# A transformer block with linear attention on one core: start-up loads on two queues, denominators spread by two loads a block, and a new order of instructions

## The chip, the core and the metric

The kernel runs on one core of a Trainium2 chip. A core has five engines that run side by side and meet through semaphores: TensorE (PE, matrix products; its weight loads, PEld, overlap them), VectorE (DVE), ScalarE (ACT), GpSimd (POOL) and SyncE (SP). Data come and go by DMA: SP, ACT and POOL each issue transfers from a queue of their own, and the core's 16 DMA engines carry them out. The metric is the device time of one execution in microseconds (us). The kernel before took 738.85 us (median of three runs, 738.4 to 741.09).

## The reference

One block of a transformer for 2,048 rows of width 1,024: a modulation vector from c, a normalized attention part with 32 heads of width 32 and linear attention, and a normalized feed-forward part of width 3,584. All arrays are bfloat16.

```python
x = A_x
mod = (silu(c) @ w_mod).reshape(c.shape[0], 6, 1, -1)
sa, ca, ga, sb, cb, gb = (mod[:, i] for i in range(6))
h = layernorm(x) * (1 + ca) + sa
# attention: q, k, v = h @ wqkv, 32 heads of width 32
#   pq, pk = phi(q), phi(k);  phi(t) = where(t > 0, t + 1, exp(t)) + 1e-6
#   kv = sum over rows of pk (outer) v;  z = sum over rows of pk
#   o = (pq @ kv) / (pq . z + 1e-6);  result = o @ wo
x = x + ga * attention(h)
h = layernorm(x) * (1 + cb) + sb
x = x + gb * ((gelu(h @ w_gate) * (h @ w_up)) @ w_down)
```

## The kernel before

**Tiling.** The 2,048 rows are four blocks of 512 rows (b = 0 to 3), each four tiles of 128 rows; the feed-forward part works on two groups of 1,024 rows. The width of 1,024 is eight column groups of 128 (`KD`), each with four heads. Most products of 512 rows or more are made with seven sub-products in place of eight (`seven`), which costs sums on VectorE.

**Who decides the order.** The kernel's text doesn't issue instructions. `Plan` records them, with their engine and what they read and write, and `order` then schedules each engine's list by a model of costs. After that `refine` moves each engine's instructions by the table `SHIFTS`: one number for each instruction, saying from how many places further on the one in this place is taken. `issue` emits the result. Each engine and each queue runs its list strictly in order, so an instruction that waits holds up all behind it.

**The start** (`start_phase`). SP loads four tiles of x (line 772), quarters of the weights Wv (line 776) and halves of two column sets of `w_mod` (line 939), after a first DMA for c (line 767). Tiles 0, 1 and 3 get their statistics on VectorE (`ln_rows`: two bn_stats, line 857, one bn_aggr, line 859, and Ln and Exp on ScalarE); tile 2 gets them on ScalarE (`act_stats`, lines 876 to 879). The tiles are normalized (lines 886 and 982), transposed on TensorE (`start_tile`, line 899), and copied to `hs0` (lines 902 and 903). Meanwhile c becomes `scol` (lines 965 to 971 and one product at line 779), and `scale_cols` (line 924) makes the columns `opcA` (line 927) by which `scale_wv` (line 907) scales Wv. Then the V products run (`v_plain`, line 915), and `keep_warm` (line 893) puts two products without a use in between. ScalarE's function table is loaded once, at line 759, before everything else on ScalarE.

**The denominators.** `den_sums(pr, ps)` makes the 32 heads' denominators for two blocks (pr 0: blocks 0 and 1; pr 1: blocks 2 and 3) with 16 small products (line 1271), turns them into reciprocals on ScalarE (lines 1273 and 1274) and stores them in DRAM (`den_scr`, four stores of 16 KB, line 1279). `den_mul(b)` loads them back with each head's row repeated on 32 partitions (line 1289) into `rden`, 128 x 8 x 512, and VectorE multiplies the block's `pqT[b]` by them, two column groups at a time (a product at line 779). Blocks 0, 1 and 2 share one buffer `rden`; block 3 has another.

**What follows.** `wo_tile` makes the output projection of blocks 0 and 1, tile by tile (16 products at line 1519, an addition to x at line 1521 that frees the banks); `wo_stages` makes blocks 2 and 3 with `seven` (line 1583). ScalarE and VectorE normalize each tile (line 1461), GpSimd stores it, SP loads it back transposed (line 1455), and the feed-forward part begins (lines 1698, 1709). In between TensorE makes modulation rows from `w_mod` (`ModSet`, loads at line 788, products at line 796).

The two parts of `den_mul` and `den_sums` that move data, as they stand:

```python
sy.dma_start(out=den_scr[pr][b, :, KH * half:KH * half + KH, 0:TG], in_=rdc[o:o + KH * P // DH, :])
...
for j in range(P // DH):
    src = den_scr[b // 2][b % 2, j][:, 0:TG]
    sy.dma_start(out=rden[DH * j:DH * j + DH], in_=src[None, :, :].to_broadcast((DH, KD, TG)))
```

Of the kernel before, what the change touches and what calls it, by code (L numbers as in the profile page):

```python
# [11 lines left out]
BF16 = mybir.dt.bfloat16  # L12
# [4 lines left out]
ACT_TABLE_LN_EXP = 6  # L17
# [4 lines left out]
        "z1 4 4 4 4 4 -5 -5 -5 -5 48 -1 -1 -1 -1 -1 -1 -1 -1 -1 -1 -1 -1 -1 -1 -1 -1 7 7 7 7 7 7 7 7 7 7 7 7 7 7 7 7 "  # L22
        "-17 -17 -17 -17 -17 -17 -17 -17 3 3 3 3 -5 -5 -5 -5 8 8 8 8 20 20 20 20 20 20 20 20 20 20 20 20 20 20 20 20 "
        "-20 -20 -20 -20 24 24 24 24 24 24 24 24 24 24 24 24 24 24 24 24 -28 -28 -28 -28 -28 -28 -28 -28 -44 -44 -44 "
        "-44 16 16 16 16 -36 -36 -36 -36 12 12 12 12 12 12 12 12 12 12 12 12 -8 -8 -8 -8 -36 -36 -36 -36 28 28 28 28 "
        "-40 -40 -40 -40 -4 -4 -4 -4 z16 -20 -20 -20 -20 z12 16 16 16 16 16 16 16 16 16 16 16 16 16 16 16 16 16 16 16 "
        "16 16 16 16 16 16 16 16 16 16 16 16 16 -24 -24 -24 -24 -24 -24 -24 -24 -40 -40 -40 -40 -40 -40 -40 -40 8 8 8 8 "
        "8 8 8 8 8 8 8 8 8 8 8 8 -16 -16 -16 -16 -16 -16 -16 -16 z8 16 16 16 16 16 16 16 16 16 16 16 16 16 16 16 16 -16 "
        "-16 -16 -16 -16 -16 -16 -16 8 8 8 8 52 -21 -21 -21 -21 -21 -21 -21 -21 -1 -1 -1 -1 -1 -1 -1 -1 11 11 11 11 11 "
        "11 11 11 28 28 28 28 19 19 19 19 11 11 11 11 20 20 20 20 -25 -25 -25 -25 -25 -25 -25 -25 -25 -25 -25 -25 8 8 8 "  # L30
        "8 8 8 8 8 25 25 25 25 25 25 25 25 13 13 13 13 -37 -37 -37 -37 -37 -37 -37 -37 -3 -3 -3 -3 25 25 25 25 25 25 25 "
        "25 25 25 25 25 25 25 25 25 -32 -8 -8 -8 -8 -32 -32 -32 -32 -40 -40 -40 -40 -16 -16 -16 -16 -12 -12 -12 -12 -20 "
        "-20 -20 -20 40 40 40 40 z4 -8 -8 -8 -8 -4 -4 -4 -4 -4 -4 -4 -4 -4 -4 -4 -4 20 20 20 20 -4 -4 -4 -4 -12 -12 -12 "
        "-12 -8 -8 -8 -8 -8 -8 -8 -8 -8 -8 -8 -8 36 36 36 36 -4 -4 -4 -4 -4 -4 -4 -4 z4 4 4 4 4 -12 -12 -12 -12 -8 -8 "
        "-8 -8 4 4 4 4 8 8 8 8 8 8 8 8 -12 -12 -12 -12 16 16 16 16 z4 12 12 12 12 12 12 12 12 -36 -36 -36 -36 -8 -8 -8 "
        "-8 -16 -16 -16 -16 12 12 12 12 4 4 4 4 -4 -4 -4 -4 8 8 8 8 -16 -16 -16 -16 -4 -4 -4 -4 4 4 4 4 -4 -4 -4 -4 z8 "
        "4 4 4 4 -4 -4 -4 -4 4 4 4 4 -4 -4 -4 -4 z16 4 4 4 4 24 24 24 24 24 24 24 24 -4 -4 -4 -4 -4 -4 -4 -4 -20 -20 "
        "-20 -20 28 28 28 28 20 20 20 20 32 32 32 32 -20 -20 -20 -20 -20 -20 -20 -20 -20 -20 -20 -20 -12 -12 -12 -12 "
        "-12 -12 -12 -12 -12 -12 -12 -12 28 28 28 28 4 4 4 4 -12 -12 -12 -12 -12 -12 -12 -12 16 16 16 16 -4 -4 -4 -4 "
        "-12 -12 -12 -12 12 12 12 12 -8 -8 -8 -8 z4 -20 -20 -20 -20 16 16 16 16 16 16 16 16 16 16 16 16 -8 -8 -8 -8 12 "  # L40
        "12 12 12 -12 -12 -12 -12 -24 -24 -24 -24 8 8 8 8 -20 -20 -20 -20 -4 -4 -4 -4 4 4 4 4 -4 -4 -4 -4 4 4 4 4 -4 -4 "
        "-4 -4 4 4 4 4 -4 -4 -4 -4 z8 32 32 32 32 32 32 32 32 32 32 32 32 -12 -12 -12 -12 -8 -8 -8 -8 -8 -8 -8 -8 -20 "
        "-20 -20 -20 60 60 60 60 60 60 60 60 -16 -16 -16 -16 -24 -24 -24 -24 8 8 8 8 8 8 8 8 8 8 8 8 -28 -28 -28 -28 "
        "-36 -36 -36 -36 -16 -16 -16 -16 -24 -24 -24 -24 8 8 8 8 -12 -12 -12 -12 -12 -12 -12 -12 -12 -12 -12 -12 -12 "
        "-12 -12 -12 12 12 12 12 12 12 12 12 12 12 12 12 12 12 12 12 -24 -24 -24 -24 -12 -12 -12 -12 12 12 12 12 -24 "
        "-24 -24 -24 16 11 11 11 11 -9 -9 -9 -9 -9 -9 -9 -9 9 9 9 9 z5 -14 -14 -14 -14 z24 6 6 6 6 -2 -2 -2 -2 -8 -8 "
        "z10 6 6 6 6 -4 -4 -4 -4 -4 -4 2 2 2 2 2 2 2 2 -8 1 1 1 1 1 1 7 7 7 7 -18 6 6 6 6 -8 -8 -8 -8 2 -9 -9 11 11 11 "
        "11 -4 z4 1 -9 -9 -9 -9 1 1 1 1 -9 32 32 32 32 32 32 32 32 32 32 32 32 32 32 32 32 48 48 48 48 48 48 48 48 24 "
        "24 24 24 -28 -28 -28 -28 -28 -28 -28 -28 -28 -28 -28 -28 -28 -28 -28 -28 -28 -28 -28 -28 4 4 4 4 4 4 4 4 4 4 4 "
        "4 -40 -40 -40 -40 -40 -40 -40 -40 -40 -40 -40 -40 z8 64 64 64 64 4 4 4 4 4 4 4 4 -12 -12 -12 -12 -12 -12 -12 "  # L50
        "-12 4 4 4 4 4 4 4 4 -12 -12 -12 -12 -12 -12 -12 -12 -4 -4 -4 -4 -4 -4 -4 -4 -4 -4 -4 -4 -4 -4 -4 -4 4 4 4 4 4 "
        "4 4 4 -12 -12 -12 -12 -12 -12 -12 -12 z16 8 8 8 8 8 8 8 8 -8 -8 -8 -8 -8 -8 -8 -8 4 4 4 4 -4 -4 -4 -4 z8 44 44 "
        "44 44 24 24 24 24 -8 -8 -8 -8 -8 -8 -8 -8 -4 -4 -4 -4 -12 -12 -12 -12 -4 -4 -4 -4 -12 -12 -12 -12 -8 -8 -8 -8 "
        "16 16 16 16 8 8 8 8 -12 -12 -12 -12 -12 -12 -12 -12 -12 -12 -12 -12 4 4 4 4 -4 -4 -4 -4 8 8 2 2 2 2 4 4 4 4 4 "
        "4 4 4 -14 -14 -14 -14 8 8 8 8 8 8 8 8 -4 -4 -4 -4 -12 -12 -12 -12 20 20 20 20 -4 -4 -4 -4 -4 -4 -4 -4 12 12 12 "
        "12 24 24 -2 -2 -2 -2 -10 -10 -10 -10 10 10 10 10 -22 -22 -22 -22 8 8 32 32 -6 -6 -6 -6 6 6 -16 -16 -16 -16 22 "
        "22 z2 -8 -8 -8 -8 -4 -4 -4 -4 z2 -6 -6 -6 -6 z2 -6 -6 -6 -6 z4 6 6 -2 -2 -2 -2 -2 -2 6 6 6 6 -2 -2 -2 -2 4 4 4 "
        "4 -12 -12 38 38 8 8 8 8 34 34 -4 -4 -4 -4 8 8 4 4 -14 -14 -22 -22 -6 -6 -6 -6 -2 -2 -2 -2 8 8 -22 -22 20 20 20 "
        "20 -6 -6 -12 -12 -12 -12 -10 -10 -10 -10 z6 4 4 4 4 -14 -14 -14 -14 z6 12 12 12 12 -4 -4 -4 -4 32 32 32 32 8 8 "
        "8 8 -12 -12 -12 -12 -12 -12 32 32 -8 -8 -8 -8 -18 -18 8 8 24 24 -2 -2 -12 -12 -12 -12 -12 -12 -12 -12 6 6 6 6 "  # L60
        "z2 -16 -16 -16 -16 8 8 8 8 z4 6 6 6 6 z2 4 4 4 4 4 4 -30 -30 -30 -30 30 30 30 30 -2 -2 -2 -2 10 10 10 10 z2 -4 "
        "-4 -16 -16 -12 -12 -12 -12 24 24 4 4 -4 -4 16 16 -6 -6 -6 -6 -20 -20 -20 -20 z6 12 12 -12 -12 -12 -12 -2 -2 -2 "
        "-2 -2 -2 -2 -2 4 4 -2 -2 -2 -2 6 6 6 6 -4 -4 -4 -4 26 26 26 26 2 2 -10 -10 z6 26 26 -14 -14 -14 -14 22 22 2 2 "
        "-6 -6 -6 -6 -6 -6 -16 -16 -16 -16 z2 -6 -6 -6 -6 8 8 8 8 -8 -8 -8 -8 -4 -4 -4 -4 z2 6 6 6 6 36 36 -2 -2 -8 -8 "
        "-8 -8 z2 -4 -4 26 26 -4 -4 4 4 4 4 -4 -4 30 30 -6 -6 24 24 -16 -16 -16 -16 -4 -4 z2 -12 -12 -12 -12 -10 -10 "
        "-10 -10 2 2 2 2 -4 -4 -10 -10 -10 -10 50 50 -2 -2 -2 -2 2 2 -4 -4 -4 -4 -2 -2 -2 -2 -2 -2 4 4 4 4 30 30 -8 -8 "
        "-8 -8 2 2 2 2 -6 -6 -6 -6 28 28 10 10 -20 -20 24 24 -10 -10 -10 -10 -6 -6 -6 -6 -6 -6 4 4 -18 -18 -18 -18 z4 "
        "54 54 -12 -12 -12 -12 -2 -2 -2 -2 -2 -2 -2 -2 z4 8 8 8 8 -2 -2 -2 -2 8 8 -16 -16 6 6 24 24 -4 -4 -4 -4 30 30 "
        "-22 -22 -18 -18 -6 -6 -6 -6 22 22 2 2 -10 -10 -10 -10 -10 -10 -10 -10 -10 -10 z6 -10 -10 -10 -10 z10 40 40 -2 "
        "-2 -2 -2 -2 -2 34 34 2 2 2 2 -8 -8 -8 -8 4 4 z2 -6 -6 -6 -6 -2 -2 -2 -2 8 8 -4 -4 -4 -4 -4 -4 16 16 16 16 -32 "  # L70
        "-32 4 4 4 4 4 4 -6 -6 -6 -6 12 12 2 2 2 2 -26 -26 -26 -26 4 4 4 4 -6 -6 -6 -6 z2 10 10 10 10 2 2 2 2 -8 -8 -8 "
        "-8 22 22 8 8 8 8 -14 -14 16 16 -8 -8 -8 -8 -8 -8 -8 -8 20 20 -6 -6 14 14 -4 -4 -10 -10 -10 -10 -4 -4 -4 -4 -4 "
        "-4 -4 -4 -4 -4 z10 4 4 10 10 -4 -4 -4 -4 -2 -2 -2 -2 2 2 2 2 2 2 -8 -8 z2 6 6 6 6 14 14 14 14 -8 -8 -8 -8 -8 "
        "-8 -4 -4 z2 14 14 -8 -8 -8 -8 10 10 z6 8 8 8 8 10 10 10 10 4 4 8 8 8 8 8 8 -12 -12 -12 -12 4 4 -32 -32 -32 -32 "
        "z4 24 24 6 6 6 6 20 20 -4 -4 -4 -4 -12 -12 -12 -12 22 22 4 4 -8 -8 -8 -8 16 16 -10 -10 -10 -10 -10 -10 z2 -6 "
        "-6 -6 -6 8 8 8 8 -8 -8 -8 -8 -4 -4 -4 -4 2 2 2 2 10 10 10 10 34 34 -10 -10 -4 -4 -4 -4 6 6 26 26 -14 -14 -10 "
        "-10 z2 -8 -8 -8 -8 26 26 26 26 z2 -6 -6 -6 -6 z2 -16 -16 -16 -16 6 6 6 6 z2 -16 -16 -16 -16 12 12 6 6 6 6 -16 "
# [131 lines left out]
class Plan:  # L209
# [5 lines left out]

    LINE = 16

    def __init__(self, tc):
        nc = tc.nc
        self.tc, self.ops, self.calls = tc, [], {}  # L220
        self.chain, self.pairs = [], []
# [275 lines left out]
def kernel(  # L497
# [13 lines left out]
    nc = tc.nc  # L511
    P = 128
# [8 lines left out]
    TG = 512  # L521
# [1664 lines left out]
```

## Time and profile before

| | |
|---|---|
| median of three runs | 738.85 us (738.4 to 741.09) |
| the profiled execution's own time | 740.71 us |
| its span, first to last instruction | 738.9 us |
| stretch 0 to 15 us: TensorE, VectorE, ScalarE busy | 5.42, 10.79, 7.15 us; DMA share 0.90, 281 GB/s |
| stretch 15 to 31 us | 16.00, 9.45, 6.67 us; DMA share 1.07, 373 GB/s |
| stretch 170 to 190 us | 18.39, 14.28, 18.95 us; DMA share 0.89, 247 GB/s |
| stretch 200 to 222 us | 20.68, 19.14, 18.31 us; DMA share 0.97, 264 GB/s |
| stretch 245 to 300 us | 55.00, 54.46, 45.70 us; DMA share 0.65, 217 GB/s |
| stretch 720 to 738.9 us | 14.85, 15.72, 0.20 us; DMA share 0.22, 72 GB/s |
| denominator loads, line 1289 | 16 of 256 KB, issued from 175.8 to 208.1 us, 0.45 us an issue |
| denominator stores, line 1279 | 8 of 16 KB, issued from 169.4 to 202.0 us, 0.59 us an issue |

The profile is of one execution. A matmul's busy time overlaps that of the next, so TensorE can show as busy and still have short stops. The DMA share is the mean over the core's 16 DMA engines, and can go a little over 1 since a packet is counted in the stretch in which it begins.

### The profile page before, as it was taken

To read this page: it belongs to the slowest core of one execution; us is meant where nothing else is said; L and a number is where in the kernel's file an instruction comes from. 1 tells how busy PE (TensorE), PEld (TensorE's weight loads), DVE (VectorE), ACT (ScalarE), POOL (GpSimd) and SP (SyncE) were. 2 spreads that over 40 slices of the span, in tenths; PEclk is the share of its full clock that TensorE was granted. 3 is DMA by queue.
4 is the path that set the end of the run, shared out by engine and by line. 5 is a ranking of instruction groups with operands and counts; after the bars stand their busy time and mean duration, and the time that the engine had idled before them with its cause. 6 is when DMAs were issued, how large, how long until landed. Compare 5 with 4: busy or idle time off the path is not lost.

```text
span 738.9 us, 12098 instructions
## 1 busy us (share of the span) xinstructions
PE 719.7 (97%) x4341; PEld 404.2 (55%) x4353; DVE 655.2 (89%) x1469; ACT 451.6 (61%) x823; POOL 97.8 (13%) x174
## 2 busy tenths in 40 slices
PE   4999999999999999999999999999999999999997
PEld 3444444444344455555555576545555555568674
DVE  6799978787789999998998798888898999999998
ACT  4385665669787789999777631017667766753110
POOL 2345542020020101213100000101000000000000
PEclk9999999999999999999999999999999999999999
DMA  9977886986799685666795898753334546599982
GB/s 296 363 209 223 207 156 127 339 283 179 243 271 258 209 279 194 192 203 229 235 202 173 228 288 244 273 186 114 114 91 153 185 161 207 157 240 302 262 270 73
DMA packets 160956, 159.26 MB, mean 216 GB/s; under 512 B 34176, under 2 KB 140416, under 8 KB 160256
## 3 DMA queue, kind: packets, MB, share of 16 engines
q1 hardware_dynamic: 143696, 122.57, 55.9%
q0 software_dynamic: 14848, 33.82, 15.4%
q10 hardware_dynamic: 2352, 2.10, 0.9%
q8 instruction: 34, 0.56, 0.3%
q14 instruction: 26, 0.21, 0.1%
HBM read 122.42 MB, written 36.04 MB: 214 GB/s over the span
## 4 chain that ended last, share of the span: by engine, by line
PE 79%; DVE 12%; DMA 4%; ACT 2%; SPq 1%; issue 1%; DVEq 0%; ACTq 0%
PE psum L1698 33%; PE psum L1959 11%; PE psum L1709 11%; PE psum L1914 9%; DVE mem L779 8%; PE psum L1142 5%; PE psum L1583 3%; PE psum L1212 3%; DMA mem<-den 3%; PE psum L915 2%; DVE mem L857 2%; DMA den<-mem 1%; DVE mem L1062 1%; DVE mem L1081 1%; PE psum L1256 1%
## 5 line engine op out<-in xcount | busy, mean ns | idle before, releaser
L779 DVE TENSOR_TENSOR mem<-mem 128x512 f16<-128x512 f16 (+13 forms) x857 | 376.5, 485 | 15.5 <-DMA mem<-den 4.3
L1698 PE MATMUL psum<-mem 128*128 128x512 f16 x1144 | 275.0, 379 | 0.2
L1086 ACT ACTIVATE mem<-psum 128x512 f32<-128x512 f32 (+3 forms) x320 | 169.0, 556 | 131.8 <-PE psum L1959 45.2
L779 DVE TENSOR_TENSOR mem<-psum,mem 128x512 f16<-128x512 f32 (+5 forms) x213 | 159.3, 756 | 26.9 <-PE psum L1142 5.4
L1698 PEld LDWEIGHTS <-mem 128*128 128x128 f16 (+1 forms) x1144 | 111.8, 98 | 101.3 <-issue 1.5
L1709 PE MATMUL psum<-mem 128*128 128x256 f16 x742 | 108.4, 273 | 0.0
L1709 PEld LDWEIGHTS <-mem 128*128 128x128 f16 (+1 forms) x742 | 72.2, 98 | 44.9 <-DVE psum L779 0.7
L1959 PE MATMUL psum<-mem 128*128 128x256 f16 (+1 forms) x784 | 88.0, 273 | 0.0
L1959 PEld LDWEIGHTS <-mem 128*128 128x128 f16 x784 | 76.7, 98 | 11.7
L1914 PE MATMUL psum<-mem 128*128 128x512 f16 (+2 forms) x348 | 74.9, 370 | 0.6 <-DVE mem L779 0.5
L1142 PE MATMUL psum<-mem 128*128 128x512 f16 (+1 forms) x274 | 62.4, 379 | 0.4
L779 DVE TENSOR_TENSOR psum<-psum,mem 128x256 f32<-128x256 f32 x106 | 44.6, 427 | 13.4 <-ACT mem L1086 12.0
L1914 PEld LDWEIGHTS <-mem 128*128 128x128 f16 x350 | 34.2, 98 | 36.2 <-issue 0.7
L1212 PE MATMUL psum<-mem 128*128 128x512 f16 x224 | 51.7, 379 | 1.5 <-DVE mem L779 1.3
L1142 PEld LDWEIGHTS <-mem 128*128 128x128 f16 x280 | 27.1, 98 | 31.8 <-issue 0.6
L1754 ACT ACTIVATE psum<-psum 128x512 f32<-128x512 f32 x56 | 32.6, 585 | 11.8 <-PE psum L1709 7.7
L1773 ACT ACTIVATE mem<-psum 128x512 f16<-128x512 f32 x56 | 33.1, 598 | 9.1 <-PE psum L1698 9.1
L1715 ACT ACTIVATE psum<-psum 128x256 f32<-128x256 f32 x53 | 19.7, 379 | 30.5 <-PE psum L1709 30.3
L1212 PEld LDWEIGHTS <-mem 128*128 128x128 f16 (+1 forms) x224 | 21.5, 98 | 27.6 <-issue 3.1
L1783 ACT ACTIVATE mem<-mem 128x512 f16<-128x512 f16 x56 | 34.6, 627 | 1.0 <-DVE mem L779 1.0
L1519 PE MATMUL psum<-mem 128*128 128x512 f16 x128 | 28.4, 379 | 1.6 <-DVE mem L779 1.6
L1241 PE MATMUL psum<-mem 128*128 128x512 bf16 x124 | 28.2, 379 | 0.2
(142 smaller groups left out, 569.7 us busy)
## 6 DMA issues: line engine op xcount, KB each, us to landing
mem<-in_B_w_gate_dram SPq DMA_DIRECT2D x14, 1024.0 KB
mem<-in_B_w_up_dram SPq DMA_DIRECT2D x14, 1024.0 KB
mem<-in_w_mod_dram SPq DMA_DIRECT2D x24, 512.0 KB
mem<-us SPq DMA_DIRECT2D x24, 448.0 KB
mem<-ts SPq DMA_DIRECT2D x5, 1792.0 KB
ts<-in_B_w_down_dram POOLq DMA_DIRECT2D x28, 256.0 KB, 5.5
mem<-in_B_w_down_dram SPq DMA_DIRECT2D x15, 448.0 KB
mem<-in_A_x_dram SPq DMA_DIRECT2D x24, 256.0 KB
```

The costliest lines, as they stand in the source:

```text
L779: ve.tensor_tensor(out=out, in0=a, in1=b, op=op)
L1086: ac.activation(out=t, in_=ps, func=AF.Copy)
L1142: te.matmul(ps, lhsT=A[:, k, i * P:(i + 1) * P], rhs=B[:, k, :], start=(start and k == 0), stop=(k == KH - 1), skip_group_check=True)
L1212: te.matmul(o, lhsT=W[:, k, (j0 + i) * P:(j0 + i + 1) * P], rhs=h_form(a, k), start=(start and k == 0), stop=(k == KH - 1), skip_group_che ...
L1519: te.matmul(psw[:, half, :], lhsT=pqT[b][:, g, tl * P:(tl + 1) * P], rhs=Wp[:, g, half * NW:(half + 1) * NW], start=(g == 0), stop=(g == K ...
L1698: te.matmul(ps, lhsT=a[:, k, e, :], rhs=b[:, k, :], start=(start and k == 0), stop=(k == KH - 1), skip_group_check=True)
L1709: te.matmul(ps, lhsT=self.x[a][:, k, :], rhs=self.y[y][:, k, :], start=(start and k == 0), stop=(k == KH // 2 - 1), skip_group_check=True)
L1754: ac.activation(out=z, in_=x, func=AF.Copy)
L1773: ac.activation(out=o, in_=ps, func=AF.Gelu_apprx_tanh)
L1783: ac.activation(out=o, in_=o, func=AF.Gelu_apprx_tanh)
L1914: te.matmul(psm[:, q, c], lhsT=A[:, i, q * P:(q + 1) * P], rhs=wt[:, i, c], start=(start and i == 0), stop=(i == NPR - 1), skip_group_chec ...
L1959: te.matmul(ps[:, q, :], lhsT=a[:, k, q * P:(q + 1) * P], rhs=y[:, k, :], start=(start and q == 0 and k == 0), stop=(k == NPR // 2 - 1), s ...
```

## The change

Three sets of edits.

- **The start.** The loads of c, of x tiles 1 and 3 and of the first half of the first column set of `w_mod` are issued by ScalarE instead of SP. The function table is loaded in front of ScalarE's first instruction that is no DMA, so behind those four issues. Tiles 1 and 3 get their statistics on ScalarE, tiles 0 and 2 on VectorE. All 32 products of one column set (line 924 before) stand together; `keep_warm` takes a normalized tile as its operand and both its products stand behind tile 2's transposes; the V products use other banks and another order. SP's planned order no longer ties the first x load to c.
- **The denominators.** `den_scr` has rows of 4,096 elements without padding, and `den_mul` loads a block with two DMAs of 512 KB in place of four of 256 KB. One covers four column groups on all 128 partitions; its source is four rows of 2,048 elements, each repeated 32 times.
- **The table `SHIFTS`** is new for all five engines, and so the order of instructions changes from start to end. On SP the first load of `rden` for block 0 now follows three of the four stores; for blocks 2 and 3 the order is block 2's first half, block 3's second, block 3's first, block 2's second.

In the built program TensorE has the same 4,353 matmuls; VectorE has two bn_stats and one bn_aggr fewer, ScalarE four DMAs more and one tile's statistics more, SP twelve DMAs fewer.

```diff
+                if self.load_table and op.eng == "ACT" and not op.bytes:
+                    self.load_table()
+                    self.load_table = None
...
-    den_scr = [scr_pool.tile([2, P // DH, KD, TG + DH], BF16, name=f"den{pr}", tag=f"den{pr}") for pr in range(2)]
+    den_scr = [scr_pool.tile([2, P // DH, KD * TG], BF16, name=f"den{pr}", tag=f"den{pr}") for pr in range(2)]
...
-    sy.dma_start(out=c8[0:KD, :], in_=c2[0].rearrange("(k p) -> k p", p=P))
+    ac.dma_start(out=c8[0:KD, :], in_=c2[0].rearrange("(k p) -> k p", p=P))
...
-            xs.append(load_x(len(xs)))
-            order.append(plan.ops[-1])
+            xs.append(load_x(len(xs), ac if len(xs) % 2 else sy))
+            if len(xs) % 2:
+                order.append(plan.ops[-1])
...
-            sy.dma_start(out=wm_ca[h][:, k, :], in_=w_mod[...
+            (sy if h or i else ac).dma_start(out=wm_ca[h][:, k, :], in_=w_mod[...
...
-            if i == 2:
+            if i % 2:
                 nmean, rstd = act_stats(x, junk0)
...
         start_tile(halves[0], 0, xh[0])
-        keep_warm(1, NW)
         scale_cols(0, 0, KH, psc[0])
+        scale_cols(0, KH, KD, psc[0])
         start_tile(halves[1], 1, xh[1])
-        scale_cols(0, KH, KD, psc[0])
         start_tile(halves[0], 2, xh[2])
-        keep_warm(1, NW)
+        keep_warm(2, xh[1][:, 0:NW])
...
-                sy.dma_start(out=den_scr[pr][b, :, KH * half:KH * half + KH, 0:TG],
+                sy.dma_start(out=den_scr[pr][b, :, half * KH * TG:(half + 1) * KH * TG].rearrange("j (g t) -> j g t", g=KH),
                              in_=rdc[o:o + KH * P // DH, :])
...
-        plan.together(True)
-        for j in range(P // DH):
-            src = den_scr[b // 2][b % 2, j][:, 0:TG]
-            sy.dma_start(out=rden[DH * j:DH * j + DH], in_=src[None, :, :].to_broadcast((DH, KD, TG)))
-        plan.together(False)
+        for h in range(2):
+            src = den_scr[b // 2][b % 2, :, h * KH * TG:(h + 1) * KH * TG]
+            sy.dma_start(out=rden[:, h * KH:(h + 1) * KH, :].rearrange("p g t -> p (g t)"),
+                         in_=src[:, None, :].to_broadcast((P // DH, DH, KH * TG)))
```

## The prediction

> **What bounds the kernel now.** I read the page's busy times first, then TensorE's waits, then the chain that ended last, then the start and the denominators closely.
>
> ```profile
> PE 719.7 (97%) x4341; PEld 404.2 (55%) x4353; DVE 655.2 (89%) x1469; ACT 451.6 (61%) x823; POOL 97.8 (13%) x174
> PE 79%; DVE 12%; DMA 4%; ACT 2%; SPq 1%; issue 1%; DVEq 0%; ACTq 0%
> ```
>
> TensorE sets the end: it is busy 97% of the span and the change leaves its 4,353 matmuls as they are. Only time in which it stands still can be won or lost. Which waits those are, by TensorE's table of waits (line, releaser: total us, times, longest):
>
> ```profile
> PE psum L967 <- DVE mem L965: 4.2, 1, 4.2
> PE psum L899 <- DVE mem L886: 4.1, 2, 3.2
> PE psum L1583 <- DVE mem L779: 1.6, 3, 0.9
> PE psum L1519 <- DVE mem L779: 1.6, 2, 0.9
> ```
>
> The first two rows are the start, before 12.8 us. The last two are the output projection, where the products wait for VectorE to multiply by the denominators. The chain of waits (start us, us, what) says why VectorE is late there:
>
> ```profile
> 12.80 2.32 PE psum L899 x20
> ...
> 172.26 3.47 DMA den<-mem
> 177.75 9.28 DMA mem<-den
> 187.06 1.90 DVE mem L779 x3
> ...
> 200.87 3.71 DMA den<-mem
> 208.14 9.25 DMA mem<-den
> 218.19 1.68 DVE mem L779 x2
> ```
>
> Twice the end waits 3.5 us for a small store of denominators and 9.3 us for the loads that spread them. Measured start to start against its usual pace (216 ns for 512 columns, 427 ns before 17 us), TensorE loses 1.9 us at 187.8 to 190.0 and 2.1 us at 220.7 to 223.9: 4.0 us. All its stops after 15 us add up to some 17 us, most of them too short to have a name, so no edit here can win much.
>
> **The denominator loads (line 1289 before).** Before, a block takes four loads of 256 KB; the outermost dimension of both sides is 32 rows. After, it takes two of 512 KB: 128 rows at the destination, but 4 groups, each repeated 32 times, at the source. What matters is how many DMA engines share one load. The engines leave one mark each on the load's semaphore in the trace. An x tile (128 rows) leaves 16. The load of c (8 rows) leaves one at once, at 2.16, and eight from 3.98 to 4.11. The small store of denominators (16 rows into 4 groups) leaves one at 170.57 and four from 171.31 to 171.37. So the smaller outer count has set the number of engines, and I take four engines for the new loads. The other bound is 16, as for every pattern with 128 rows here.
>
> The Trainium skill ("DMA: Bandwidth & Descriptors", "Why a DMA increments its semaphore by 16 and not by 1") says that the engine count is the largest number up to 16 that divides the outermost sizes of both sides, and its rules warn of a zero-step outer dimension of few copies. The trace agrees with 5 and 9 marks; by that rule the new loads have four engines, and always the same four.
>
> What that costs, from the DMA view of 206.5 to 216 us (only denominator loads on this queue; packets, MB, share of 16 engines):
>
> ```profile
> q1 hardware_dynamic: 2049, 1.97, 100.2%
> ```
>
> 1.002 x 16 x 9.5 us / 2049 = 74 ns for a packet of 1 KB, so 64 packets an engine, 4.7 us for a block. Packets of 4 KB have a median of 159 ns in the trace (981 of them from 128 to 150 us). On four engines a load of 512 KB is 32 x 159 ns = 5.1 us and a block 10.2 us; the two blocks of the second pair take 20.4 us where they took 9.5. On 16 engines a load would be 8 x 159 ns = 1.3 us. Other loads of the queue go to all 16 engines and so stand behind these on the four.
>
> I walk it from the end of the sums (line 1271, 168.1 us) as zero, with the changed program's order on each queue. The first store is issued at 1.35 (ScalarE's two steps, as before), then loads of x and stores alternate on SP at 0.4 to 0.75 us an issue.
> - Block 0: its first load goes out at 5.2, starts on the four engines behind four x tiles at 6.7 and lands at 12.6, its second starts behind two 512 KB loads of w_mod and lands at 21.0. TensorE has 92 matmuls in between (76 of line 1212, 16 of 1301; 88 before) and four of its own: 96 x 0.216 = 20.8. It loses 0.7 us instead of 1.9: -1.2.
> - Block 1 shares its buffer with block 0, so its loads go out at 22 and start at 24.7 behind three more loads of w_mod. They land at 30.6 and 37.0; TensorE wants them at 37.6, and VectorE has five multiplications, sums and additions of 0.55 to 1.2 us queued behind the late one, one of which frees the banks of the next tile. I get 3.0 us; before, the block had landed at 199.9 with 6 us to spare: +3.0.
> - Blocks 2 and 3: the four loads start at 41.1 and land at 47.0, 52.1, 57.2 and 62.3 (before: by 49.3). VectorE's new order puts each multiplication ahead of the addition (line 1521's) that frees banks for a later tile, so TensorE stops four times: 1.3 + 2.2 + 1.6 + 1.1 = 6.2 us, less the 2.1 of before: +4.1.
> - GpSimd's stores share the four engines: 508 packets of 4 KB on its queue from 203 to 220 us, 32 an engine, 5.1 us. The old loads carried a share of it too; I add 1.5.
>
> Sum: +7.4 us. Bounds: with 16 engines it is a gain, of at most the 4.0 us lost now. With four engines and nothing hidden, 20.4 - 9.5 = 10.9 for the second pair and 3.0 for block 1: +13.9. I take +7.4, since the stores show four.
>
> SP issues eight fewer of these loads (0.45 us each): 3.6 us off a queue that waits for landings here, so nothing; if it did not wait, the second pair could start at most that much earlier. The stores keep their number and size, and that each new load needs one store's landing instead of two is in the issue times above.
>
> **The start.** Four of the first eight loads move to ScalarE's queue, ahead of the table load (1.28 us, from 0.74 to 2.02 now). Four issues of 0.43 us put the table at 2.5 to 3.8; ScalarE's first step waits for VectorE's statistics and ran at 5.05, so that cover hides it. The eight loads' bytes come to what landed by 11.32 before: six x tiles and two halves of w_mod then, four x tiles, two halves of w_mod and a quarter of Wv now, 2.5 MB each time.
>
> ```profile
> 0.00:15.00 15.00, 5.42 (x65) 4.34 (x66) 10.79 (x41) 7.15 (x17) 3.56 (x21) 1.00 0.90 281
> ```
>
> DMA (last two columns: share, GB/s) is already at 0.90 here, and issues of 0.36 to 0.51 us stand against landings 0.7 to 1.5 us apart, so a second queue adds little; I keep 11.3 for the second half of w_mod. The Trainium skill (same page, "Issuing engines are not separate DMA queues") says that two queues only save issue time; by it the gain is nothing.
>
> What changes is the order. x tile 2 stood second (landed 4.12) and now stands behind 512 KB of Wv, beside ScalarE's queue: with 2.0 MB landed, some 8.5 us. VectorE's second step of statistics waits for it, and behind that stands the copy of c (line 968), for which ScalarE's exponential waits, ahead of its Square of tile 1: 0.67 + 0.11 + 0.19 + 1.34 + 0.49 + 0.54 + 0.17 and gaps of 0.3 make 3.8, so scol at 12.3, where the second half of line 924 ran at 11.4. Then 32 of line 924 (1.2), 16 transposes (1.7) and two warm-up products (0.85), all at half pace: first V products at 16.0 against 15.38. The statistics of a second tile on ScalarE take two bn_stats and an aggregate off VectorE (1.5 us) and add 2.6 us to ScalarE, which is idle 7.9 of these 15 us. I take +0.5; bounds -1.5 (x tile 2 not late, transposes 1.5 us earlier) and +3 (x tile 2 with everything else at 11.3, or the half pace lasting longer).
>
> **The shift table** reorders every engine. From 245 to 720 us TensorE's stops come to 2.2 us: that is the most to be won there. At the tail, 0.7 us (line 1914 at 733.67). A worse order could lose as much: -3 to +3, taken as 0.
>
> **Sum.** 7.4 + 0.5 = +7.9. The profiled execution took 740.71 us (span 738.9 and 1.8 around it) and would take 748.6; the median of the runs, 738.85, becomes 746.7.
>
> **Rivals.**
> - All 16 engines: the loads are shorter than before, 2.5 us a block against 4.7, and most of the 4.0 us is won: -3 + 0.5, 736.3. For it: the destination has 128 rows. Against it: the store's five marks. This is the side faster than before; it decides if the marks of a new load are 16.
> - Four engines, but hidden: only block 1 and a part of the second pair show, +2, 740.9. For it: VectorE is busy 89%, not 100%, and pieces of its work can wait. Against it: additions that free banks stand behind the multiplications.
> - Four engines and a late start: x tile 2 at 11 us and the half pace until 19 us, 3 us more than I took: 750. For it: landings of tiles spread up to 1.7 us (5.22 to 6.89) already now.
>
> **Chances.** Forecast 0.55 (742.5 to 750), hidden 0.17 (738 to 742), 16 engines 0.13 (733 to 738), late start too 0.15 (750 to 756). From 737 to 754 some 0.83 lie. I count 0.5% (3.7 us) as what a measurement can tell: faster 0.09, within it 0.21, slower 0.70.
>
> **What would show it.** Landings: four marks and one, and a DMA row in the chain of some 20 us after 205 us. TensorE's waits at lines 1519 and 1583 should grow from 3.2 to 10 us or so; line 899 or 924's should hardly shrink, and the first x4 of line 915 should begin at 15 to 17 us. I am wrong if the new loads' time from issue to landing is below 5 us, or if the products of line 1583 begin less than 2 us later against line 1271 than now.

## The result and the profile after

The changed kernel takes 766.06 us (median of four runs, 764.48 to 767.23) against 738.7: a ratio of 1.0362, 95% interval 1.0331 to 1.0392. It is slower, as forecast, but by 27 us and not by 8, and outside the range. The page's busy times and the chain's shares:

```profile
PE 727.8 (95%) x4353; PEld 406.1 (53%) x4353; DVE 652.0 (85%) x1466; ACT 453.2 (59%) x827; POOL 99.0 (13%) x174
PE 74%; DMA 12%; DVE 10%; SPq 2%; ACT 1%; issue 1%; DVEq 0%; ACTq 0%
```

TensorE is busy 8.1 us longer with the same 4,353 matmuls, and its share has still fallen. DMA's share of the chain has tripled. TensorE's waits (line, releaser: total us, times, longest):

```profile
PE psum L1526 <- DVE mem L787: 12.0, 5, 5.2
...
PE psum L1590 <- DVE mem L787: 4.6, 3, 2.6
PE psum L1220 <- DVE mem L787: 3.0, 1, 3.0
PE psum L931 <- DVE mem L787: 2.5, 1, 2.5
```

Lines have moved by 7 to 9: 1526 and 1590 are the output projection (1519 and 1583 before), 1220 is line 1212, 931 is line 924. The output projection stops for 16.6 us where it stopped for 3.2, and TensorE now stops even ahead of it, at line 1220. Line 931 stands in the start. The others wait for VectorE to multiply, and VectorE's own table says for what it waits, before (165 to 225 us) and after:

```profile
DVE mem L779 <- DMA mem<-den: 4.3, 3, 2.2
```

```profile
DVE mem L787 <- DMA mem<-den: 31.3, 7, 7.7
```

The chain of waits (start us, us, what) shows the loads one behind the other:

```profile
174.71 17.73 DMA mem<-den
193.78 11.14 DMA mem<-den
204.94 12.29 DMA den<-mem
217.89 19.68 DMA mem<-den
238.20 3.02 DVE mem L787 x4
```

Before, it held a store of 3.5 us and loads of 9.3 us, twice. Now there are 17.7, 11.1 and 19.7 us of loads, and a store of 16 KB that takes 12.3 us to land.

Every new load leaves five marks on its semaphore, one at about 1 us from issue and four when data lands: four engines. How full they are can be read from the DMA view where little else runs, at 188 to 193 us (packets, MB, share of 16 engines):

```profile
q1 hardware_dynamic: 137, 0.52, 25.6%
```

25.6% of 16 engines is 4.1: four engines without a pause, 12 idle, 0.10 MB a us.

To see where the time went, I took TensorE's lost time: the moment, less what the products begun so far take at full pace (216 ns for 512 columns and in proportion, a quarter of it for products into 32 rows). The few matmuls missing from a trace are filled in from the program's order. In us, for the two kernels and for three of the experiments below:

```
at us    before   after   b_four  a_wide  a_split
30        14.6     14.2    14.4    14.2    14.2
80        15.3     15.3    14.9    15.3    14.9
160       17.6     15.7    16.3    15.7    15.2
200       20.3     25.0    25.9    16.2    15.7
220       20.8     32.9    30.1    20.8    15.9
240       22.5     40.8    40.8    22.5    15.8
260       22.6     45.9    50.3    22.6    15.9
400       23.8     47.0    51.8    25.1    18.4
end       25.5     48.9    53.5    26.9    20.4
```

From 160 to 260 us the changed kernel loses 30.2 us and the kernel before 5.0. All the rest of the change is within 2 us. The two executions traced, on which the views rest, have spans of 738.9 and 762.7 us: they are 23.8 us apart, the medians 27.

### The profile page after: what moved, and what is told of

It reads as the page before. It is cut to its first block, busy times and chain, and to the rows that moved or that the text cites. A ratio compares the mean times of both kernels' runs of the same rounds, so it can differ in the third digit from the quotient of the medians.

```text
span 762.7 us, 12086 instructions
## 1 busy us (share of the span) xinstructions
PE 727.8 (95%) x4353; PEld 406.1 (53%) x4353; DVE 652.0 (85%) x1466; ACT 453.2 (59%) x827; POOL 99.0 (13%) x174
## 4 chain that ended last, share of the span: by engine, by line
PE 74%; DMA 12%; DVE 10%; SPq 2%; ACT 1%; issue 1%; DVEq 0%; ACTq 0%
PE psum L1705 31%; PE psum L1716 11%; PE psum L1150 8%; PE psum L1966 7%; DVE mem L787 7%; PE psum L1921 7%; DMA mem<-den 6%; PE psum L1220 4%; DMA mem<-in_A_wqkv_dram 3%; PE psum L1590 3%; PE psum L1249 2%; DMA den<-mem 2%; PE psum L1264 1%; DVE mem L1900 1%; DVE mem L2131 1%
## 5 line engine op out<-in xcount | busy, mean ns | idle before, releaser
L787 DVE TENSOR_TENSOR mem<-mem 128x256 f16<-128x256 f16 (+11 forms) x857 | 376.9, 483 | 48.3 <-DMA mem<-den 31.3
L1705 PE MATMUL psum<-mem 128*128 128x512 f16 x1144 | 273.5, 379 | 0.0
L1094 ACT ACTIVATE mem<-psum 128x256 f32<-128x256 f32 (+3 forms) x320 | 167.4, 555 | 130.2 <-PE psum L1966 38.0
L1966 PEld LDWEIGHTS <-mem 128*128 128x128 f16 x784 | 76.7, 98 | 12.9 <-issue 0.5
L1220 PE MATMUL psum<-mem 128*128 128x512 f16 x224 | 53.7, 386 | 3.0 <-DVE mem L787 3.0
L1526 PE MATMUL psum<-mem 128*128 128x512 f16 x128 | 34.0, 428 | 12.0 <-DVE mem L787 12.0
L1590 PE MATMUL psum<-mem 128*128 128x512 f16 x112 | 26.8, 397 | 4.6 <-DVE mem L787 4.6
L1526 PEld LDWEIGHTS <-mem 128*128 128x128 bf16 x128 | 13.5, 107 | 32.6 <-issue 12.7
```

What stands on the lines that cost most here:

```text
L787: ve.tensor_tensor(out=out, in0=a, in1=b, op=op)
L1094: ac.activation(out=t, in_=ps, func=AF.Copy)
L1220: te.matmul(o, lhsT=W[:, k, (j0 + i) * P:(j0 + i + 1) * P], rhs=h_form(a, k), start=(start and k == 0), stop=(k == KH - 1), skip_group_che ...
L1526: te.matmul(psw[:, half, :], lhsT=pqT[b][:, g, tl * P:(tl + 1) * P], rhs=Wp[:, g, half * NW:(half + 1) * NW], start=(g == 0), stop=(g == K ...
L1590: te.matmul(ps, lhsT=A[:, k, i * P:(i + 1) * P], rhs=B[:, k, :], start=(start and k == 0), stop=(k == KH - 1), skip_group_check=True)
L1705: te.matmul(ps, lhsT=a[:, k, e, :], rhs=b[:, k, :], start=(start and k == 0), stop=(k == KH - 1), skip_group_check=True)
```

## The experiments

Each kernel is made from before or after, and its table `SHIFTS` is written anew so that every engine's order stays as it was, but for what the edit adds or takes. Ratios are to the kernel before on the same chip.

**Undoing the loads alone, and doing them alone.** `a_wide` is the changed kernel with four loads a block:

```diff
-        for h in range(2):
-            src = den_scr[b // 2][b % 2, :, h * KH * TG:(h + 1) * KH * TG]
-            sy.dma_start(out=rden[:, h * KH:(h + 1) * KH, :]..., in_=src[:, None, :].to_broadcast((P // DH, DH, KH * TG)))
+        for j in range(P // DH):
+            src = den_scr[b // 2][b % 2, j]
+            sy.dma_start(out=rden[DH * j:DH * j + DH]..., in_=src[None, :].to_broadcast((DH, KD * TG)))
```

> The changed kernel, its order of instructions kept; only the denominator loads are again four a block, one for each group of 32 partitions (rows of 8 KB), all four at the place of the block's first load. If the four engines cost the loss, by themselves and by what stands behind them, it takes 733 to 740 us (about 736: 1.4 us won at the start, 1 to 2 us at the output projection). If the new order costs it, it stays above 755. If the loads cost only the 7.4 us of the prediction, about 758.

`b_four` is the kernel before with the change's edit of the denominators alone (the last two hunks of the diff and the scratch's shape).

> The kernel before, start and order kept; only the scratch without padding and the two 512 KB loads a block, in the places of the first and third of four. If the four engines cost the loss, 755 to 770 us (about 764). By the prediction's own sum, 738.85 + 7.4 = 746. If the new order of the changed kernel costs it, 739 to 743.

Measured: a_wide 742.99 us, ratio 1.0047 (1.0027 to 1.0067); b_four 767.64, ratio 1.0378 (1.0343 to 1.0413). In the order of before the two new loads of each block lose the whole 28 us by themselves; in the order of after, taking them out wins 23 of the 27. The new order is not the cause, and the prediction's 7.4 us is not the size. b_four's chain has the same rows as that of after:

```profile
174.35 18.40 DMA mem<-den
196.88 14.52 DMA mem<-den
215.75 28.52 DMA mem<-den
```

a_wide did miss the 733 to 740 us that I expected, and stays 0.5% slower than before. Its loads land 3.3 to 8.9 us after issue in the second pair, but each covers all columns of 32 partitions, so that VectorE's first multiplication waits for the last of four; in the changed order it comes early. VectorE still waits, and TensorE behind it (VectorE's row, then TensorE's):

```profile
DVE mem L787 <- DMA mem<-den: 8.9, 3, 4.7
```

```profile
PE psum L1534 <- DVE mem L787: 4.2, 2, 2.7
```

**Only the outermost count.** `a_split` keeps the halves, the 4 KB rows and the places, and cuts each load into the four groups of 32 partitions:

```diff
         for h in range(2):
-            src = den_scr[b // 2][b % 2, :, h * KH * TG:(h + 1) * KH * TG]
-            ...
+            for j in range(P // DH):
+                src = den_scr[b // 2][b % 2, j, h * KH * TG:(h + 1) * KH * TG]
+                sy.dma_start(out=rden[DH * j:DH * j + DH, h * KH:(h + 1) * KH, :]..., in_=src[None, :].to_broadcast((DH, KH * TG)))
```

> The changed kernel with each of its eight denominator loads cut into four, one for each group of 32 partitions: the same rows of 4 KB, the same places in SP's order and the same halves of the buffer, 24 DMA issues more. Only the outermost count changes, from 4 to 32. If the number of engines is the cause, 740 to 747 us, near a_wide's 743. If the length of the rows (4 KB here, 8 KB in a_wide), the halves or the order are the cause, it stays above 755.

Measured: 736.9 us, ratio 0.9966 (0.9952 to 0.9981): faster than both kernels, and better than I expected. The same bytes in the same rows, now in eight loads of 128 KB a block, leave 16 marks for each load and land 3.7 to 4.4 us after issue in the second pair, where the loads of 512 KB took 9.1 to 26.5. With 24 more issues on SP, VectorE waits 1.5 us for these loads in place of 31.3, and TensorE runs through the output projection (start us, us, what):

```profile
184.49 5.34 PE L1529 MATMUL psum<-mem 128*128 128x512 f16 x24
...
192.58 22.62 PE L1529 MATMUL psum<-mem 128*128 128x512 f16 x104
215.03 1.89 PE L1593 MATMUL psum<-mem 128*128 128x512 f16 x8
```

104 products in 22.62 us is 217 ns each: no stop. The same stretch of 100 us in three kernels, before, b_four and a_split in this order (TensorE busy is the second number after the stretch, the granted clock the one ahead of the last two):

```profile
160.00:260.00 100.00, 96.78 (x511) 43.44 (x510) 87.11 (x151) 76.41 (x122) 9.81 (x18) 1.00 0.82 244
```

```profile
160.00:260.00 100.00, 75.59 (x370) 31.45 (x369) 58.48 (x99) 54.54 (x86) 6.46 (x12) 0.86 0.66 173
```

```profile
160.00:260.00 100.00, 100.00 (x534) 46.88 (x532) 90.20 (x162) 81.48 (x133) 9.07 (x16) 1.00 0.86 246
```

b_four makes 370 products where before makes 511 and a_split 534.

**Which block.** Three kernels give a_wide's loads to some blocks and leave the others the two of after.

> The changed kernel with block 1's loads alone on all engines (four loads of 256 KB); blocks 0, 2 and 3 keep the two loads on four engines. If the loads are one chain on the four engines, in which block 1's loads (landed 11.1 and 19.6 us after issue) hold back the second pair's stores (12.3 us to land) and so all that follows, some 10 us are won: about 756. If each block has a price of its own, as in the prediction, block 1's 3.0 us: 763. If block 1 is hidden behind the rest, 766.

> The changed kernel with the loads of blocks 0 and 1 on all engines; blocks 2 and 3 keep two loads on four. By TensorE's lost time (17 us from 160 to 220 us, 13 from 220 to 260) some 14 us are won: about 752. By the prediction's terms for the blocks (block 0 won 1.2, block 1 lost 3.0) 2 us: 764.

> The changed kernel with the loads of blocks 2 and 3 on all engines; blocks 0 and 1 keep two loads on four. By TensorE's lost time from 220 to 260 us some 11 us are won: about 755; if pieces add up, this gain and that of a_wide01 make 23 us, the whole way to a_wide. If the second pair's wait only takes the place of the first pair's, the two gains together are clearly less than 23 us. By the prediction's term for the second pair, 4.1 us and GpSimd's 1.5: 760.

Measured: block 1 wide 759.51 us (ratio 1.0266, 1.0241 to 1.0292); blocks 0 and 1 wide 748.48 (1.0123, 1.0098 to 1.0147); blocks 2 and 3 wide 762.16 (1.0301, 1.0275 to 1.0328). Against the 1.0362 of after, and with 1% as 7.4 us: block 1 wide wins 7.1 us, the first pair wide 17.7, the second pair wide 4.5. Seen from a_wide's 1.0047, the second pair alone on four engines costs 5.6 us and the first pair alone 18.8; both together cost 23.3. Each of these differences has an interval of some 2.5 us either way, so the two add up as far as these runs can tell. I had the first of these too small (14 expected) and the second too large (11). With the second pair wide, the chain still carries the first (start us, us, what):

```profile
174.81 19.85 DMA mem<-den
197.13 17.28 DMA mem<-den
214.43 5.13 DMA den<-mem
222.82 8.78 DMA mem<-den
```

With block 1 wide, the store in the chain takes 5.4 us in place of 12.3: the stores of the second pair had been queued behind block 1's second load.

**Other engines.** In `a_gp` the loads of after keep their shape, and GpSimd issues them:

```diff
-            sy.dma_start(out=rden[:, h * KH:(h + 1) * KH, :]...
+            gp.dma_start(out=rden[:, h * KH:(h + 1) * KH, :]...
```

> The changed kernel with its eight denominator loads, unchanged in shape, issued by GpSimd in front of its first store of normalized rows. If the loss comes from four engines that are always the same for SP's queue, so that the loads, the small stores and every other load's share line up on them, and GpSimd's loads spread over other engines, 742 to 755 us. If GpSimd's loads of this shape go to the same four, about 766. If one load's own 5.1 us on four engines is what costs, whichever they are, 755 to 766.

Measured: 757.48 us, ratio 1.0268 (1.0223 to 1.0313), 7 us better than after; three runs lie from 756.5 to 757.5 us and one at 765.04. It falls where I had put "one load's own 5.1 us on four engines". The two loads of block 1 land 14.6 and 15.8 us after issue, together, and not 11.1 and 18.6, one behind the other; the second pair's small stores need 1.8 to 5.3 us, not 12.3 to 12.9. So the lining up on SP's four engines fits as part of the loss (block 0's loads also go out 2 us earlier here). A load is still slow, and the rest of the loss stays.

On this queue each of these loads leaves 16 marks, but they come in groups. Block 1's first load has twelve by 199.7 us and four from 208.60 to 208.79. Its second has eight by 199.9 us, four from 208.84 to 209.00, just behind those of the first, and four from 209.12 to 210.67. That fits four engines for each load, and not the same four. From 198 to 203 us the two run alone, side by side:

```profile
q0 software_dynamic: 118, 0.48, 51.1%
```

51.1% of 16 engines is 8.2. Yet eight engines move 0.10 MB a us, no more than four did for one load alone in after, and their packets of 4 KB have a median of 325 ns in place of 159. That is why two loads at once took 15 us; what halves the pace is open.

**Half pace.** After its longer stops TensorE starts again at half pace. The granted clock is the third number from the right:

```profile
185.00:190.00 5.00, 4.78 (x15) 0.66 0.62 192
...
215.00:220.00 5.00, 3.47 (x8) 0.50 0.25 92
```

In all TensorE is busy for 17.6 us at half pace, which loses 8.8 us; that accounts for the 8.1 us of longer busy time. In `a_warm` products without a use fill two of the stops:

```diff
         psw = banks.pair()
+        for _ in range({4: 20, 7: 11}.get(tt, 0)):
+            te.matmul(psm[:, 4, :], lhsT=ident, rhs=Wp[:, 0, 0:NW], start=True, stop=True, skip_group_check=True)
```

> The changed kernel with 31 products without a use on TensorE: 20 ahead of the products that stop for 5.2 us at 216 us, 11 ahead of those that stop for 3.1 us at 233 us, as long as the stops and not longer. If the half pace after a stop adds to the time, the two lose 2.0 and 1.6 us by the granted clock and 3.6 us are won: about 762.4. If the loads' landings set this stage's end, what is won at full pace is waited for at the next load: within 1 us of the changed kernel's 766.

Measured: 764.19 us, ratio 1.0339 (1.0309 to 1.0368), whose interval overlaps that of after. The fillers did their work (the x20 of line 1525; start us, us, what):

```profile
209.93 4.48 PE L1525 MATMUL psum<-mem 128*128 128x512 f16 x20
214.94 1.02 PE L1528 MATMUL psum<-mem 128*128 128x512 f16 x4 [0.52 <-DVE mem L787]
217.34 6.22 PE L1528 MATMUL psum<-mem 128*128 128x512 f16 x28 [1.38 <-DVE mem L787]
225.56 5.30 PE L1528 MATMUL psum<-mem 128*128 128x512 f16 x16 [2.00 <-DVE mem L787]
```

The stop of 5.17 us is down to 0.52, and the four products behind it take 1.02 us in place of 1.86. But the next stops grow, from 0.54 to 1.38 and from 0.98 to 2.00 us, and the 2.00 brings a new half pace. The second pair's last load takes 26.54 us to land, against 26.53. TensorE is now busy for 9.9 us at half pace: the fillers took away 3.9 us of its loss. By the ratios 1.7 us were won, with an interval of some 3 us either way, which the runs can't tell from nothing. The grown stops show that a part of the half pace lies in time that would have been waited for anyway; how much is not shown, and the half pace that is left was not tried.

**The start alone.** `b_start` is the kernel before with the change's edits of the start and their order, and then the order of before; `b_start_wide` adds 8 KB rows to its four loads.

> The kernel before with the changed kernel's start alone: its two queues, statistics, banks and order up to the last instruction of the start on each engine, and then the order of before. By the traces (the first product of line 859 at 26.74 us where it was at 28.16) 1.4 us are won: about 737.4 us. By the prediction's term for the start, 0.5 us are lost: 739.3. If what is won at the start is lost at the next wait for a load, no change: 738.8.

> The kernel of b_start, and its four denominator loads a block with rows of 8 KB in place of eight rows of 1 KB, on all engines. If the time of the loads' packets (74 ns a KB in 1 KB rows, 159 ns for 4 KB) is what the output projection waits for, 2 to 3 us less than b_start: about 735. If the wait is for issue and landing of a chain of small steps, within 1 us of b_start.

Measured: 745.31 us (ratio 1.0079, 1.0052 to 1.0106) and 744.5 (1.0074, 1.0046 to 1.0102). These tell little of the start, since the seam between the two orders is bad. From 40 to 60 us TensorE stops behind it, for instance (last bracket: idle time, releaser):

```profile
49.49 0.68 PE L1264 MATMUL psum<-mem 128*128 128x129 f16 x9 [1.27 <-ACT mem L1256]
51.18 3.49 PE L1249 MATMUL psum<-mem 128*128 128x512 bf16 x8 [1.01 <-DVE mem L1070]
55.85 0.34 PE L1264 MATMUL psum<-mem 128*128 128x129 f16 x3 [1.17 <-ACT mem L925]
```

b_start's lost time goes from 16.2 at 40 us to 21.9 at 60, where it stays near 15 in before and in after; b_start_wide, with the same seam, does as b_start. The 8 KB rows won 0.8 us of the 2 to 3 expected, and the intervals overlap: nothing that can be told. The expectation's 1.4 us were misread too: the first product of line 859 is earlier because the orders differ, not because TensorE has lost less. The table of lost time says 0.4 us won at 30 us and nothing at 80.

**The rows alone, in before.** `b_split` and `b_wide` are the kernel before with a_split's loads, and with rows of 8 KB.

```diff
-            src = den_scr[b // 2][b % 2, j][:, 0:TG]
-            sy.dma_start(out=rden[DH * j:DH * j + DH], in_=src[None, :, :].to_broadcast((DH, KD, TG)))
+            src = den_scr[b // 2][b % 2, j]
+            sy.dma_start(out=rden[DH * j:DH * j + DH]..., in_=src[None, :].to_broadcast((DH, KD * TG)))
```

> The kernel before, start and order kept, with a_split's loads: eight of 128 KB for a block, rows of 4 KB, by halves of the columns, two in each place of one. If the halves and rows alone make a_split's gain (0.34%), 2 to 3 us faster than before: about 736.5. If the gain comes from the changed kernel's order, which multiplies as soon as a half is there, within 1 us of before or a little slower by the issues: 739 to 741.

> The kernel before, its four loads a block with rows of 8 KB in place of eight rows of 1 KB; nothing else. If the packets' time (64 of 74 ns an engine for a block, against 8 of about 309) is what TensorE waits for at the output projection, where it loses 5 us from 160 to 260 us, 2 to 3 us faster: about 736.5. If issue, landing and the chain of steps make the wait, within 1 us of before: 739.

Measured: 737.11 us (ratio 0.9973, 0.9958 to 0.9987) and 737.83 (0.9977, 0.996 to 0.9994). Both gain about 1.8 us, at or just under the 2 to 3 expected, and the scratch without padding, which both need, is worth having. TensorE's waits at the output projection, 3.2 us before, are down to 0.3 us in b_wide and not in b_split's table at all. How much of it the 1 KB packets had cost is not shown: the second pair's loads took 11.3 us from the first issue to the last landing in b_wide against 12.7 before, where the packets' times promised half, and they also went out 2.1 us earlier after the sums. b_split and a_split have the same loads, and differ in all else that the change does, start and order. Their intervals overlap almost wholly (0.5 us between them, some 1.5 either way), so start and table together are worth nothing that these runs can tell.

## Why the prediction was right and wrong

**Right: the four engines.** They were read from the five marks of the small stores, and the eight new loads leave five each. The rule of the Trainium skill that the prediction cited ("DMA: Bandwidth & Descriptors", "Why a DMA increments its semaphore by 16 and not by 1") agrees: five marks at an outermost count of 4, 16 marks in a_split at 32.

**Right: the second pair by itself.** The prediction gave it 4.1 us and 1.5 for GpSimd's stores; with the first pair out of the way it costs 5.6, by a_wide01 against a_wide. That the two numbers are equal is partly luck: the 5.6 has an interval of some 2.5 us either way, and in a_wide01 the four loads landed 9.3, 14.9, 21.5 and 29.2 us after the first was issued, where the walk has them land 5.9, 11.0, 16.1 and 21.2 us after their start.

**Wrong: the first pair.** Its terms were -1.2 for block 0 and +3.0 for block 1, together +1.8; measured, by a_wide23 against a_wide, 18.8 us. The walk from the end of the sums went wrong from its first landing on. In us from that end (165.3 in the trace of after):

```
                          walked               measured
block 0, loads out        5.2                  6.1
block 0, loads landed     12.6, 21.0           18.2, 27.2
block 1, loads out        22                   28.5
block 1, loads landed     30.6, 37.0           39.7, 48.2
pair 2, loads out         41.1 (their start)   50.4
pair 2, loads landed      47.0 to 62.3         59.4 to 80.0
```

Three steps failed.
- "On four engines a load of 512 KB is 32 x 159 ns = 5.1 us." This holds where such a load runs alone: from 188 to 192 us the trace's packets of 4 KB have a median of 159 ns. From 178 to 181 us, while other loads keep all 16 engines busy, the median is 274 to 300, and block 0's first load needs the time from 173 to 183.5 us. The DMA view of 178 to 182 us:

```profile
q1 hardware_dynamic: 263, 0.96, 101.0%
```

All 16 engines are full and move 0.24 MB a us, where the walk needs 0.41 (16 packets of 4 KB in 159 ns). That they are full is not by itself the reason. The 159 ns were read in before, and from 135 to 145 us there the loads of `w_mod` and of the output projection's weights fill all 16 engines while packets of 4 KB have that median:

```profile
q1 hardware_dynamic: 1419, 3.52, 97.9%
```

In a_gp, on the other hand, two denominator loads side by side had 325 ns with half of the engines idle. So a figure read from other loads was carried over to these, and it did not hold beside other traffic. Why is open.
- "The stores keep their number and size." So they do, but they use the same four engines as the loads in front of them. The second pair's first three stores needed 12.3 to 12.9 us to land, against 1.8 to 3.7 before, since block 1's second load stood ahead of them. That is 9 us on the chain that the walk doesn't have. a_wide1 shows its worth: with block 1's loads on 16 engines the store in the chain takes 5.4 us, and 7.1 us are won, in which block 1's own wait is contained.
- "... its loads go out at 22 and start at 24.7 behind three more loads of w_mod." Every load of SP's queue has four of its 16 shares on these engines, and one of x (512 KB, for block 2 or 3) is issued between block 1's two. From the first issue to the last landing block 1 took 19.7 us, the walk 15.0. How the shares line up is seen on the load of w_mod issued at 171.97 us: 12 marks from 175.8 to 176.7, and four from 182.0 to 184.5, when block 0's first load is through.

The upper bound, +13.9, added up the loads' own times. It could not hold a queue that also delays the stores that the next loads wait for. A longer chain behind one resource has no such bound; it should have been walked store by store.

**Not priced: half pace.** TensorE's 8.1 us of longer busy time at a lower clock are in the profile and not in the sum. In a_warm taking 3.9 us of the clock's loss away won nothing that the runs can tell; whether the rest is a cost of its own is not shown.

**The start.** The term was +0.5, bounds -1.5 to +3. Measured by lost time, 0.4 us are won at 30 us and none at 80. Its steps were off: the columns' product was put at 12.3 us and V's first at 16.0, and the trace has them at 11.02 and 14.38 (start us, us, what):

```profile
11.02 0.99 PE L931 MATMUL psum<-mem 128*128 128x1 bf16 x32 [2.50 <-DVE mem L787]
...
14.38 1.69 PE L922 MATMUL psum<-mem 128*128 128x512 f16 x4
```

The walk let x tile 2 wait for its place in the bytes, until 8.5 us; it was there 0.9 us earlier. The bytes were miscounted too: five x tiles, and not six, had landed by 11.32 us before, 2.25 MB with the two halves of w_mod. That TensorE began 1.0 us earlier with V is worth little, since what lost time it saved came back by 80 us.

**The table** was taken as 0, and a_split against b_split says 0.

**The rivals.** "All 16 engines" was given 736.3 us, on the ground that the loads would then be hidden. For the change as written it was wrong, but for a_split, whose loads do leave 16 marks, it came within 1 us (736.9). That close it is partly luck: the rival has 2.5 us for a block, and a_split's landings in the second pair, 0.50 us apart for each 128 KB, make it 4.0. "Four engines, but hidden" and "late start too" are out.

## What to carry to other kernels

Count a load's engines from the outermost counts of both its sides before counting its bytes: the same 4 MB of loads cost 28 us with an outermost count of 4 (b_four) and won 2 us with 32 (b_split). A transfer on few engines also delays the share that every later transfer of the queue has on them, small stores included; so walk the queue as one chain and follow what the next load waits for. Lost time against the full pace, stage by stage, tells where a change acts; the start of one instruction doesn't, when the order has changed.

## What was not expected of the hardware

- A packet of 4 KB took 159 ns with 12 engines idle (188 to 192 us in after) and also with all 16 busy (135 to 145 us in before), but 270 to 300 ns where a denominator load stood beside loads of w_mod, and 325 ns where two denominator loads ran on eight engines. Whether the sources, of which the engines read the same rows 32 times, or something else makes it slower was not tried.
- TensorE fell to half pace after stops of 2.0 us (225.56 in a_warm: 0.66 from 225 to 230 us) and 2.3 us (193.2 in after), and not after 1.0 us (226.6 in after: 1.00). The Trainium skill ("TensorE: Matmul & The Clock Gate", "Part 1: The HAM clock gate (the 'warmup' mystery)") gives an idle window of about 3.4 us for that; the trace differs, with shorter stops. In the traces of after, a_warm and b_four the granted clock changes at moments that lie multiples of 3.41 us apart, and half pace begins where TensorE was busy for 0 to 1.41 us of the 3.41 us before such a moment; with 1.71 us and more it did not. Two neighbours from after and two from a_warm (TensorE busy is the second number after the stretch, the granted clock the third from the right):

```profile
189.79:193.20 3.41, 1.16 (x6) 1.00 0.26 105
193.20:196.61 3.41, 3.40 (x9) 0.50 0.29 102
```

```profile
243.12:246.53 3.41, 1.72 (x9) 1.00 0.99 191
246.53:249.95 3.42, 3.42 (x18) 1.00 1.21 271
```

- SP's semaphores for DMAs are used again after eight, and the issue waits for the earlier landing: a load of w_mod at 183.53 us waited for block 0's first load, landed at 183.5, after SP had begun no other issue since 175.83. One slow load holds up the queue that way too.
